# Attention and a routed expert layer on one core: the first units' plan cut in seven pieces, seven copies moved to ScalarE, four subtracts to GpSimd

## The chip, the cores and the metric

The kernel runs on one core of a Trainium2 chip. Its time is device microseconds from one execution, and several executions of the same program are shown. A core has TensorE (PE; its weight loads are shown apart as PEld), VectorE (DVE), ScalarE (ACT), GpSimd (POOL) and SyncE (SP), which only issues transfers here. Each engine works through its own queue in order, and waits by semaphores for what others produce. Lower is better.

## What is computed

Attention over 4 sequences of 768 tokens with 8 heads of 64, in which a token sees the 96 tokens up to itself and 8 global ones; then each of the 3072 rows of 512 goes to the one of 8 experts that a small gate chooses, and is multiplied by its gate weight:

```python
scores = scale * q @ k.T - slope * dist          # kept: is_global | is_local
a = softmax(scores); x = (a @ v) as rows [3072, 512]
logits = x @ w_gate + modality_bias[modality_id]
e_idx = argmax(logits); gate_w = softmax(logits)[e_idx]
for e in range(8):
    out[e_idx == e] = gate_w * (relu(x[e_idx == e] @ w1[e]) @ w2[e])
```

All is float32. w1 is 8 x 512 x 1024 and w2 is 8 x 1024 x 512.

## The kernel before

**Attention** goes over 24 blocks of 128 tokens (NBLK), 6 to a sequence (NB), in steps n = 0 to 24 of the function `step`. A step is a software pipeline: it makes the scores of block n on TensorE (`s_mm`), reduces them on VectorE with the bias table (`red`, L276, name sc) and exponentiates them on ScalarE (L287, pr); it transposes the probabilities of block n-1 on TensorE (`t_mm`, L301, tile pt, four pairs of heads, two PSUM buffers) and copies them to SBUF (`t_cp`, tile pT: pairs 0, 2 and 3 on VectorE, L310, pair 1 on ScalarE, L308); it multiplies by the values of block n-2 (`pv`), scales them (`rinv`, tile rin, L345; `xr`) and stores them in the DRAM buffer x_rows; and it transposes the queries and keys of block n+1 (`k_mm`, `k_cp`: qt on VectorE, kt on ScalarE, L228). GpSimd copies value rows meanwhile (`copyv`, L135, L137, L142: vo, vl).

**Routing.** The gate (`gate_a`, `gate_b`, `gate_c`) runs one to two steps later. When a sequence is complete, `route_a` to `route_d` give each token a place in a list sorted by expert: pks and pos (positions; the adds run on GpSimd, L427 to L433, but for the last sequence), pf and pi (as integers, VectorE), and `route_c` scatters the tokens to the DRAM list ids_sorted by indirect transfers from GpSimd's queue (L450), six to a sequence.

**Experts.** A unit is 256 rows of one expert. Its matmuls work on numbers split in a high and a low part: `split` makes of the raw weights a rounded copy on ScalarE (L661, ah for w1, bh for w2) and the remainder on VectorE (L662, al, bl), four pieces of 128x1024 for each matrix. `l1_unit` multiplies by w1 in groups of twelve matmuls, four pieces times three products (L690 to L692, phe); the last of the twelve reads the fourth piece's low part. `l2` multiplies by w2.

The first three units (eslots, NE = 3) are filled from the first two sequences alone, so that they can start before attention ends. Their **plan** needs the counts of these sequences: which expert each unit has (uei), from which place of the list (uoi), which rows are empty (inv), and how many units each expert has used (first_used, needed only by the later plan). `plan_e` runs it in four parts, by `items` and `slots`, on VectorE at the ends of steps 17, 18, 18 and 19 (LAST = 18). Then the weights of unit 0 are loaded (`ld_w`, SP's queue), the units' row numbers (`ld_x`, tile ui), and the rows gathered (`gather_x`, L628, xge, GpSimd's queue).

**What sets the order.** The dictionary `todo` holds what is done at the end of which step (`at(n, f)`). For TensorE, and in attention for ScalarE and VectorE, the order is as written. For GpSimd and SP a scheduler sets it at build time, by its own estimate of when things are ready. After step 24 the first groups of unit 0 are written among the last blocks' work (`l1_first`), then a loop runs over all units.

Of the kernel before, what the change touches and what calls it, by code (L numbers as in the profile page):

```python
# [67 lines left out]
def moe_attention_kernel(ctx, tc, q, k, v, n_global, n_local, modality, w_gate, mod_bias, w1, w2, out):  # L68
# [396 lines left out]
        scat.append(ins)  # L465


    def items(tag, pool, cnt, used, ni, first):

        def pl(name, shape, dt=F32):
            return pool.tile([P] + shape, dt, name=f"{name}{tag}")

        left = cnt
        if used is not None:
            left = pl("left", [E])
            V.scalar_tensor_tensor(left, used, -float(U), cnt, ALU.mult, ALU.add)
        ci = pl("ci", [E], I32)
        V.tensor_copy(ci, left)  # L480
        full = pl("full", [E])
        V.tensor_scalar(ci, ci, 8, None, ALU.logical_shift_right)
        V.tensor_copy(full, ci)
        t88 = pl("t88", [E, E])
        V.tensor_tensor(t88, le, bm(full, E), ALU.mult)
        cin = pl("cin", [E])
        V.reduce_sum(cin, t88, axis=AX.X)
        cex = pl("cex", [E])
        V.tensor_sub(cex, cin, full)
        if first:  # L490

            V.tensor_scalar(first_used, cex, -1.0, float(first), ALU.mult, ALU.add)
            V.tensor_scalar(first_used, first_used, 0.0, None, ALU.max)
            V.tensor_tensor(first_used, first_used, full, ALU.min)
        yield
        uc = bc(uidx[:, 0:ni], E)
        m1 = pl("m1", [ni, E])
        m2 = pl("m2", [ni, E])
        st = pl("st", [ni, E])
        V.tensor_tensor(m1, bm(cin, ni), uc, ALU.is_gt)  # L500
        V.tensor_tensor(m2, bm(cex, ni), uc, ALU.is_gt)
        V.tensor_sub(m1, m1, m2)
        V.tensor_tensor(st, uc, bm(cex, ni), ALU.subtract)
        V.tensor_mul(st, st, m1)
        yield
        if not first:
            rem = pl("rem", [E])
            V.scalar_tensor_tensor(rem, full, -float(U), left, ALU.mult, ALU.add)  # L508
            key = pl("key", [E])
            V.scalar_tensor_tensor(key, rem, 8.0, erev, ALU.mult, ALU.add)  # L510
            V.tensor_tensor(t88, bm(key, E), bc(key, E), ALU.is_gt)
            rr = pl("rr", [E])
            V.reduce_sum(rr, t88, axis=AX.X)
            V.tensor_scalar(rr, rr, cin[:, E - 1 : E], None, ALU.add)
            V.tensor_scalar(key, rem, 0.0, 1000.0, ALU.is_equal, ALU.mult)
            V.tensor_add(rr, rr, key)
            yield
            V.tensor_tensor(m2, bm(rr, ni), uc, ALU.is_equal)
            V.tensor_add(m1, m1, m2)
            V.tensor_tensor(m2, m2, bm(full, ni), ALU.mult)  # L520
            V.tensor_add(st, st, m2)
            if used is not None:
                V.tensor_tensor(m2, m1, bm(used, ni), ALU.mult)
                V.tensor_add(st, st, m2)
            yield
# [129 lines left out]
    def split(s, which, c, early=False):  # L655
        raw = s.raw.pop((which, c))
        nb = 2 if which == "b" and s.straight else 1
        pool = wspb if which == "b" or early else wsp
        th = pool.tile([P, 1024], F32R, tag=f"{which}h{c}{early}", name=f"{which}h{s.name}{c}", bufs=nb)
        tl = pool.tile([P, 1024], F32R, tag=f"{which}l{c}{early}", name=f"{which}l{s.name}{c}", bufs=nb)  # L660
        nc.scalar.copy(th, raw)  # L661
        V.tensor_sub(tl, raw, th.bitcast(F32))  # L662
# [262 lines left out]
    def at(n, f, *args):  # L925
        todo.setdefault(n, []).append((f, args))
# [135 lines left out]
    eslots, slist, grs = [], [], []  # L1062
    moe = {}

    def planned_e(r):
        uei, uoi, inv = slots("e", plan, *r, NE, 2)
        for u in range(NE):
            eslots.append(mk(f"e{u}", uei[0:1, u : u + 1], uoi[0:1, u : u + 1], inv[:, :, u], xd[0 : BE * S, :], 2))

    def plan_e(g=[]):  # L1070
        if not g:
            g.append(items("e", plan, base[:, BE - 1, NB, :], None, NE, NE))
        run("e", g[0], planned_e)

    for j in range(4):
        at(LAST - 1 + (0, 1, 1, 2)[j], plan_e)

    def open_moe():
        nonlocal wraw, wsp, xgp, idp, mp
# [8 lines left out]
    at(LAST + 1, open_moe)  # L1088
    at(LAST + 1, lambda: ld_w(eslots[0], "a", (0, 1)))
    at(LAST + 2, lambda: ld_w(eslots[0], "a", (2, 3)))  # L1090
    at(LAST + 3, lambda: [ld_x(s) for s in eslots])
    at(LAST + 4, lambda: [gather_x(s) for s in eslots[:GE]])
    for j in range(4):
        at(LAST + (3, 4, 5, 6)[j], split, None, "a", j)
# [26 lines left out]
    def step(n):  # L1121

        on, more, back = n < NBLK, n + 1 < NBLK, 0 < n <= NBLK
        load(n)
        if on:
            s_mm(n, 0)
            s_mm(n, 1)
            if not n:
                k_mm(1, 0)
                k_mm(1, 1)  # L1130
            for hh in (0, 2, 1, 3, 4, 6, 5):
                red(n, hh)
                if not n and hh == 3:
                    k_cp(1, 0)
                    k_cp(1, 1)
        if n > 1:
            rinv(n - 2)
            pv(n - 2)
        if back:
            t_mm(n - 1, 0)  # L1140
            t_cp(n - 1, 0)
            t_mm(n - 1, 1)
            t_cp(n - 1, 1, True)
        if on:
            red(n, 7)
        if n > 1:
            xr(n - 2)
        if n > 2:
            gate_a(*gates(n - 3))
        if back:  # L1150
            t_mm(n - 1, 2)
            t_cp(n - 1, 2)
        if more and n:
            k_mm(n + 1, 1)
            k_mm(n + 1, 0)
            k_cp(n + 1, 1)
            k_cp(n + 1, 0)
        if back:
            t_mm(n - 1, 3)
            t_cp(n - 1, 3, not on)  # L1160
            copyv(n - 1)
        if n > 3:
            gate_c(*gates(n - 4))
        for f, args in todo.pop(n, []):
            if f is split:
                args = (eslots[0],) + args[1:]
            f(*args)
        if n > 2:
            gate_b(*gates(n - 3))
# [26 lines left out]
    def rest():  # L1196
        for n in sorted(todo):
            for f, args in todo[n]:
                f(*args)
                if f is not route_c or args[1] == NB - 1:  # L1200
                    yield
        r = yield from items("b", plan, base[:, B - 1, NB, :], first_used, NI, 0)
        uei, uoi, inv = slots("b", plan, *[t[:, 0:NS] for t in r], NS, 2)
        for u in range(NS):
            slist.append(mk(f"s{u}", uei[0:1, u : u + 1], uoi[0:1, u : u + 1], inv[:, :, u], xd, 2))
        yield
        gr = yield from granules(*r)
# [170 lines left out]
```

## Time and profile before

| | |
|---|---|
| runs shown | 502.31, 501.94, 502.28 us, median 502.28 |
| profiled execution | 504.03 us, its span 502.2 us |
| mean granted TensorE clock | 0.987 |
| busy: PE, DVE, ACT, POOL | 468.6, 343.1, 297.5, 156.3 us |
| steps 17 to 24 | about 125 to 185 us |
| first matmul of unit 0 | 188.33 us |

Times in rows of the profile are microseconds from the start of the span. In a row of the timeline stand start, length, engine, line, operation, what it writes and reads, its shape, and in square brackets how long the engine stood idle before it and what ended that. "issue" means that the profile shows nothing that it waited for.

### The profile page before, as it was taken

The page shows a single profiled execution, that of the slowest core. Times are in us where ns is not written, and L with a number is a line of the kernel's source. Part 1 is how long each engine was busy: PE and PEld are TensorE (multiplying, and loading weights), DVE is VectorE, ACT ScalarE, POOL GpSimd, SP SyncE. Part 2 cuts the span into 40 slices and gives each one's busy share as a digit, 9 for nine tenths or more (in the row PEclk, how much of TensorE's full clock was granted, in tenths as well). Part 3 has the DMA queues.
Part 4 walks back from the last instruction along what each step waited for, and adds up shares of the span by engine and source line. Part 5 has one row for each costly group of instructions (what it writes and reads, how often), then busy time and mean ns, then how long its engine had stood idle before and what let it go on. Part 6 is the DMA issues. An engine that isn't in the chain of part 4 may idle for free.

```text
span 502.2 us, 15068 instructions
## 1 busy us (share of the span) xinstructions
PE 468.6 (93%) x5789; PEld 419.4 (84%) x5789; DVE 343.1 (68%) x999; ACT 297.5 (59%) x716; POOL 156.3 (31%) x234
## 2 busy tenths in 40 slices
PE   7879899999898989999999999899999999999991
PEld 6778899999787869898989898798988998798980
DVE  5868788978987874997756477474765748556530
ACT  6747777777667763546456466464665557555420
POOL 9513314545443355062130405204041040500100
PEclk9989999999989999999999999999999999999997
DMA  9778878787668934767785849778598666965100
GB/s 175 152 215 206 200 168 215 180 196 192 158 160 248 287 128 150 265 188 246 232 277 199 275 154 325 246 220 292 159 332 269 205 248 218 321 225 165 44 22 26
DMA packets 125509, 102.75 MB, mean 205 GB/s; under 512 B 96283, under 2 KB 97715, under 8 KB 125428
## 3 DMA queue, kind: packets, MB, share of 16 engines
q1 hardware_dynamic: 120660, 88.65, 60.8%
q0 software_dynamic: 4768, 13.05, 7.2%
q8 instruction: 47, 0.77, 0.6%
q14 instruction: 34, 0.28, 0.2%
HBM read 87.31 MB, written 14.63 MB: 203 GB/s over the span
## 4 chain that ended last, share of the span: by engine, by line
PE 44%; issue 12%; DVE 2%; DMA 2%; POOL 1%; ACT 0%; SPq 0%; POOLq 0%; DVEq 0%; ACTq 0%
PE phs L692 5%; PE phs L690 4%; PE phs L691 4%; PE pos L730 4%; PE pos L729 4%; PE pos L728 4%; PE phe L690 2%; PE phe L691 2%; PE phe L692 2%; PE poe L728 2%; PE poe L730 2%; PE poe L729 2%; DMA uig<-ids_sorted 2%; POOL out L744 1%; PE mts L673 1%
## 5 line engine op out<-in xcount | busy, mean ns | idle before, releaser
L287 ACT ACTIVATE pr<-sc,nmx 128x168 f32<-128x168 f32 x192 | 81.1, 423 | 30.5 <-DVE nmx L276 29.4
L692 PE MATMUL phs<-xhs,als 128*128 128x256 f32 x256 | 72.5, 283 | 0.6 <-DVE als L662 0.5
L690 PE MATMUL phs<-xhs,ahs 128*128 128x256 f32 x256 | 72.2, 282 | 0.0
L691 PE MATMUL phs<-xls,ahs 128*128 128x256 f32 x256 | 72.1, 282 | 0.0
L628 POOL DMA_INDIRECT xgs<-x_rows,uis x16 | 27.1, 1694 | 131.5 <-DMA uis<-ids_sorted 66.9
L276 DVE CUSTOM_DVE_ANT_0 sc<-s,tbl 128x168 f32<-128x168 f32 x192 | 52.1, 327 | 9.4 <-PE s L257 9.4
L697 DVE SCALAR_TENSOR_TENSOR hls<-phs,hhs 128x512 fp32r<-128x512 f32 x32 | 22.1, 692 | 51.0 <-ACT hhs L696 51.0
L301 PE MATMUL pt<-ident,pr 128*128 128x128 f32 x288 | 47.2, 288 | 7.3 <-DVE pT L310 4.7
L728 PE MATMUL pos<-bhs,hhs 128*128 128x512 f32 x128 | 51.4, 401 | 0.0
L730 PE MATMUL pos<-bhs,hls 128*128 128x512 f32 x128 | 50.6, 395 | 0.0
L729 PE MATMUL pos<-bls,hhs 128*128 128x512 f32 x128 | 50.5, 395 | 0.0
L692 PEld LDWEIGHTS phs<-xhs,als 128*128 128x128 f32 x256 | 48.8, 191 | 1.0 <-DVE als L662 1.0
L310 DVE COPY pT<-pt 128x384 f32<-128x384 f32 x71 | 38.9, 548 | 15.5 <-PE pt L301 15.4
L690 PEld LDWEIGHTS phs<-xhs,ahs 128*128 128x128 f32 x256 | 48.9, 191 | 0.4
L691 PEld LDWEIGHTS phs<-xls,ahs 128*128 128x128 f32 x256 | 48.8, 191 | 0.3
L696 ACT ACTIVATE hhs<-phs 128x512 fp32r<-128x512 f32 x32 | 19.1, 597 | 50.0 <-PE phs L692 50.0
L257 PEld LDWEIGHTS s<-kt,qt 64*64 64x64 f32 x1536 | 38.2, 132 | 10.4 <-ACT kt L228 6.1
L257 PE MATMUL s<-kt,qt 64*64 64x128 f32 (+1 forms) x1536 | 41.7, 248 | 4.7 <-ACT kt L228 1.8
L301 PEld LDWEIGHTS pt<-ident,pr 128*128 128x128 f32 x288 | 32.4, 144 | 13.1 <-DVE pT L310 5.4
L450 POOL DMA_INDIRECT ids_sorted<-tki,pi x24 | 25.4, 1060 | 34.7 <-DVE remb L508 17.6
L287 ACT ACTIVATION_READ_ACCUMULATOR pr<-sc,nmx 128x1 f32 x192 | 35.9, 187 | 0.0
L744 POOL DMA_INDIRECT out<-obs,ois x16 | 17.1, 1069 | 47.7 <-ACT obs L743 44.6
(343 smaller groups left out, 1251.2 us busy)
## 6 DMA issues: line engine op xcount, KB each, us to landing
va<-in_v SPq DMA_DIRECT2D x25, 256.0 KB, 4.2
kn<-in_k SPq DMA_DIRECT2D x24, 256.0 KB, 4.0
qn<-in_q SPq DMA_DIRECT2D x24, 256.0 KB, 5.0
x_rows<-xr SPq DMA_DIRECT2D x24, 256.0 KB, 3.7
vl<-in_v SPq DMA_DIRECT2D x84, 32.0 KB, 3.0
rawe0a<-in_moe_w SPq DMA_DIRECT2D x4, 512.0 KB, 5.9
rawe0b<-in_moe_w SPq DMA_DIRECT2D x4, 512.0 KB
rawe1a<-in_moe_w SPq DMA_DIRECT2D x4, 512.0 KB, 3.5
```

The lines of the kernel that those rows point to most:

```text
L257: nc.tensor.matmul(ps[h][64 * half : 64 * half + 64, c : c + cnt], qt[hs, hp, 64 * half : 64 * half + 64], keys, start=True, stop=True,)
L276: V.tensor_tensor_reduce(out=sc, in0=pss[n, hp // 2][h][:, hp % 2 * W : (hp % 2 + 1) * W], in1=(tbl0 if n % NB == 0 else tbl)[:, hh, :], o ...
L287: last[0] = nc.scalar.activation(pr[:, h * (PRW - W) : h * (PRW - W) + W], sc, AF.Exp, bias=nmx[:, hh : hh + 1], scale=-1.0, accum_out=sum ...
L301: nc.tensor.transpose(tp[:, j * P : (j + 1) * P], pr[:, o : o + P], ident)
L310: V.tensor_copy(pT.rearrange("p a b -> p (a b)"), tp[:, 0 : 3 * P])
L628: nc.gpsimd.indirect_dma_start(out=s.xg[:, t, :], out_offset=None, in_=s.xsrc, in_offset=bass.IndirectOffsetOnAxis(ap=s.ui[:, t, 0:1], axi ...
L690: nc.tensor.matmul(o, hi[:, fs], s.xh[:, c, :], start=(c == 0), stop=False)
L691: nc.tensor.matmul(o, hi[:, fs], s.xl[:, c, :], start=False, stop=False)
L692: nc.tensor.matmul(o, lo[:, fs], s.xh[:, c, :], start=False, stop=(c == 3))
L728: nc.tensor.matmul(s.po[t], s.hh[:, fc, tt], hi[:, wv], start=(fc == 0), stop=False)
L729: nc.tensor.matmul(s.po[t], s.hh[:, fc, tt], lo[:, wv], start=False, stop=False)
L730: nc.tensor.matmul(s.po[t], s.hl[:, fc, tt], hi[:, wv], start=False, stop=(fc == 7))
```

## The change

The plan of the first units is a function of its own now, in seven pieces with a `yield` behind each. Pieces 1, 3, 5 and 7 run at the ends of steps 17, 18, 19 and 21, and pieces 2, 4 and 6 in the middle of steps 18, 19 and 20, between the values' products of block n-2 and the first transposes' copy. The units are made as soon as their experts are known, and their list places and empty rows are filled in later. In steps 9, 11, 15 and 17 to 20 the third pair's copy goes to ScalarE. The low part of the four w1 pieces of unit 0 is subtracted by GpSimd. The text asks for the row numbers one step earlier.

```diff
     def split(s, which, c, early=False):
...
         nc.scalar.copy(th, raw)
-        V.tensor_sub(tl, raw, th.bitcast(F32))
+        (nc.gpsimd if which == "a" and s is eslots[0] else V).tensor_sub(tl, raw, th.bitcast(F32))
...
-    def planned_e(r):
-        uei, uoi, inv = slots("e", plan, *r, NE, 2)
-        for u in range(NE):
-            eslots.append(mk(f"e{u}", uei[0:1, u : u + 1], uoi[0:1, u : u + 1], inv[:, :, u], xd[0 : BE * S, :], 2))
-    def plan_e(g=[]):
-        if not g:
-            g.append(items("e", plan, base[:, BE - 1, NB, :], None, NE, NE))
-        run("e", g[0], planned_e)
-    for j in range(4):
-        at(LAST - 1 + (0, 1, 1, 2)[j], plan_e)
+    def plan_e():
...
+        V.tensor_copy(ci, cnt)
+        V.tensor_scalar(ci, ci, 8, None, ALU.logical_shift_right)
+        V.tensor_copy(full, ci)
+        V.tensor_tensor(t88, le, bm(full, E), ALU.mult)
+        V.reduce_sum(cin, t88, axis=AX.X)
+        yield
+        V.tensor_sub(cex, cin, full)
...
+        V.tensor_tensor(m1, bm(cin, NE), uc, ALU.is_gt)
+        V.tensor_tensor(m2, bm(cex, NE), uc, ALU.is_gt)
+        V.tensor_sub(m1, m1, m2)
+        yield
...
+        V.tensor_tensor(m2, m1, bm(eidx, NE), ALU.mult)
+        V.reduce_sum(uex, m2, axis=AX.X)
+        V.tensor_copy(uei, uex)
+        for u in range(NE):
+            eslots.append(mk(f"e{u}", uei[0:1, u : u + 1], None, None, xd[0 : BE * S, :], 2))
+        yield
+        V.tensor_tensor(st, uc, bm(cex, NE), ALU.subtract)
+        V.tensor_mul(st, st, m1)
+        V.reduce_sum(ust, st, axis=AX.X)
+        V.tensor_scalar_mul(ust, ust, float(U))
+        yield
+        V.scalar_tensor_tensor(uof, uex, float(NT), ust, ALU.mult, ALU.add)
+        V.tensor_copy(uoi, uof)
...
+        yield
+        V.tensor_scalar(first_used, cex, -1.0, float(NE), ALU.mult, ALU.add)
+        V.tensor_scalar(first_used, first_used, 0.0, None, ALU.max)
+        V.tensor_tensor(first_used, first_used, full, ALU.min)
+        yield
...
+        V.tensor_tensor(m2, m1, bm(cnt, NE), ALU.mult)
+        V.reduce_sum(uli, m2, axis=AX.X)
+        V.tensor_scalar(inv[:, 0, :], ust, pidx, None, ALU.add)
+        V.tensor_scalar(inv[:, 1, :], ust, pidx, 128.0, ALU.add, ALU.add)
+        V.tensor_tensor(inv, inv, bm(uli, 2), ALU.is_ge)
+        V.tensor_scalar_mul(inv, inv, OOB)
...
+        yield
+    parts_e = plan_e()
+    mid = {}
+    at(LAST - 1, next, parts_e)
+    mid[LAST] = mid[LAST + 1] = mid[LAST + 2] = lambda: next(parts_e)
+    at(LAST, next, parts_e)
+    at(LAST + 1, next, parts_e)
+    at(LAST + 3, next, parts_e)
+    ACT2 = {NB + 3, NB + 5, 2 * NB + 3, 2 * NB + 5, LAST, LAST + 1, LAST + 2}
...
-    at(LAST + 3, lambda: [ld_x(s) for s in eslots])
+    at(LAST + 2, lambda: [ld_x(s) for s in eslots])
...
+        if n in mid:
+            mid[n]()
         if back:
             t_mm(n - 1, 0)
             t_cp(n - 1, 0)
...
-            t_cp(n - 1, 2)
+            t_cp(n - 1, 2, n in ACT2)
```

`items` loses its branch for the first units, and is otherwise as before.

How this moves the queues is shown at two places. The first is VectorE at the end of step 17 and the start of step 18; se, pf and pi belong to the routing, cie to first_used to the plan, sc18 are the scores of block 18. Before:

```order
L444 CAST pi1_3287<-pf1_3285 128x6
L480 CAST cie_3289<-base_208 128x8
L482 TENSOR_SCALAR cie_3289<-cie_3289 128x8
L483 CAST fulle_3291<-cie_3289 128x8
L485 TENSOR_TENSOR t88e_3294<-le_205,fulle_3291 128x64
L487 TENSOR_REDUCE cine_3296<-t88e_3294 128x8
L489 TENSOR_TENSOR cexe_3298<-cine_3296,fulle_3291 128x8
L492 TENSOR_SCALAR first_used_209<-cexe_3298 128x8
L493 TENSOR_SCALAR first_used_209<-first_used_209 128x8
L494 TENSOR_TENSOR first_used_209<-first_used_209,fulle_3291 128x8
L276 ISA sc18_0_3357,nmx18_3356<-s18_0_0_3319,tbl0_169 128x168
```

VectorE with the change, from the same pi on:

```order
L444 CAST pi1_3287<-pf1_3285 128x6
L1068 CAST cie_3289<-base_208 128x8
L1069 TENSOR_SCALAR cie_3289<-cie_3289 128x8
L1070 CAST fulle_3290<-cie_3289 128x8
L1071 TENSOR_TENSOR t88e_3291<-le_205,fulle_3290 128x64
L1072 TENSOR_REDUCE cine_3292<-t88e_3291 128x8
L276 ISA sc18_0_3353,nmx18_3352<-s18_0_0_3315,tbl0_169 128x168
```

Four of nine instructions of the plan no longer stand ahead of the scores of step 18; cexe is in the second piece and first_used in the sixth. The second piece, on VectorE in the middle of step 18, behind the seventh score and rin:

```order
L345 TENSOR_SCALAR rin16_3374<-sums16_2978 128x8
L346 RECIPROCAL rin16_3374<-rin16_3374 128x8
L1074 TENSOR_TENSOR cexe_3293<-cine_3292,fulle_3290 128x8
L1077 TENSOR_TENSOR m1e_3412<-cine_3292,uidx_204 128x24
L1078 TENSOR_TENSOR m2e_3413<-cexe_3293,uidx_204 128x24
L1079 TENSOR_TENSOR m1e_3412<-m1e_3412,m2e_3413 128x24
L310 COPY pT17_0_3422<-pt17_0_3418 128x384
```

The copy of the first transposes (pT17_0), which stood right behind rin, has four instructions ahead of it.

The second place is GpSimd's queue from step 22 to the end of attention: vo are value rows, base and pos the third sequence's positions, ids_sorted the scatters (pi2 the third sequence's, pi3 the fourth's), xge2 the rows of unit 2, ale00 to ale03 the four low parts of unit 0. Before:

```order
L135 COPY vo1_81<-va2_78 64x512
L137 COPY vo1_81<-va1_77 64x512
L135 COPY vo2_82<-va3_79 64x512
L137 COPY vo2_82<-va2_78 64x512
L427 TENSOR_TENSOR base_208<-base_208,pks2_4262 128x8 x6
L431 TENSOR_TENSOR pos2_4271<-pks2_4262,base_208 128x48
L429 COPY base_208<-base_208 128x8
L432 TENSOR_TENSOR pos2_4271<-pos2_4271,ebase_202 128x48
L433 TENSOR_TENSOR pos2_4271<-pos2_4271,oh2_4053 128x48
L450 DMA ids_sorted<-tki_206,pi2_4445 24832x16 x6
L628 DMA xge2_4758<-x_rows,uie2_4086 128x512 x2
L450 DMA ids_sorted<-tki_206,pi3_4900 24832x16 x6
```

GpSimd with the change (ale00 stands between the second and the third copy, just ahead of these rows):

```order
L137 COPY vo2_82<-va2_78 64x512
L427 TENSOR_TENSOR base_208<-base_208,pks2_4262 128x8 x2
L656 TENSOR_TENSOR ale01_4282<-rawe0a1_3688,ahe01_4281 128x1024
L427 TENSOR_TENSOR base_208<-base_208,pks2_4262 128x8 x4
L431 TENSOR_TENSOR pos2_4271<-pks2_4262,base_208 128x48
L429 COPY base_208<-base_208 128x8
L432 TENSOR_TENSOR pos2_4271<-pos2_4271,ebase_202 128x48
L433 TENSOR_TENSOR pos2_4271<-pos2_4271,oh2_4078 128x48
L656 TENSOR_TENSOR ale02_4448<-rawe0a2_3865,ahe02_4447 128x1024
L450 DMA ids_sorted<-tki_206,pi2_4445 24832x16 x6
L622 DMA xge2_4758<-x_rows,uie2_3900 128x512 x2
L656 TENSOR_TENSOR ale03_4538<-rawe0a3_3867,ahe03_4537 128x1024
```

Four subtracts have come into the queue: two ahead of the positions' end, one behind it, and the fourth behind the six scatters of pi2 and the two gathers of unit 2. TensorE's order is unchanged.

More of the change, by code (lines that the diff above doesn't have):

```diff
@@ L465, in route_c, with items @@
         scat.append(ins)
-    def items(tag, pool, cnt, used, ni, first):
+    def items(tag, pool, cnt, used, ni):
         def pl(name, shape, dt=F32):
@@ L489, in items @@
         V.tensor_sub(cex, cin, full)
[L490 to L494, printed above, removed]
         yield
@@ L505, in items @@
         yield
[L506 to L520, printed above, removed]
+        rem = pl("rem", [E])
+        V.scalar_tensor_tensor(rem, full, -float(U), left, ALU.mult, ALU.add)
+        key = pl("key", [E])
+        V.scalar_tensor_tensor(key, rem, 8.0, erev, ALU.mult, ALU.add)
+        V.tensor_tensor(t88, bm(key, E), bc(key, E), ALU.is_gt)
+        rr = pl("rr", [E])
+        V.reduce_sum(rr, t88, axis=AX.X)
+        V.tensor_scalar(rr, rr, cin[:, E - 1 : E], None, ALU.add)
+        V.tensor_scalar(key, rem, 0.0, 1000.0, ALU.is_equal, ALU.mult)
+        V.tensor_add(rr, rr, key)
+        yield
+        V.tensor_tensor(m2, bm(rr, ni), uc, ALU.is_equal)
+        V.tensor_add(m1, m1, m2)
+        V.tensor_tensor(m2, m2, bm(full, ni), ALU.mult)
+        V.tensor_add(st, st, m2)
+        if used is not None:
+            V.tensor_tensor(m2, m1, bm(used, ni), ALU.mult)
             V.tensor_add(st, st, m2)
[L522 to L525, printed above, removed]
+        yield
         ust = pl("ust", [ni])
@@ L1063, in moe_attention_kernel, with pl @@
     moe = {}
-    def planned_e(r):
-        uei, uoi, inv = slots("e", plan, *r, NE, 2)
-        for u in range(NE):
-            eslots.append(mk(f"e{u}", uei[0:1, u : u + 1], uoi[0:1, u : u + 1], inv[:, :, u], xd[0 : BE * S, :], 2))
-    def plan_e(g=[]):
-        if not g:
-            g.append(items("e", plan, base[:, BE - 1, NB, :], None, NE, NE))
-        run("e", g[0], planned_e)
-    for j in range(4):
-        at(LAST - 1 + (0, 1, 1, 2)[j], plan_e)
+    def plan_e():
+        def pl(name, shape, dt=F32):
+            return plan.tile([P] + shape, dt, name=f"{name}e")
+        cnt = base[:, BE - 1, NB, :]
+        ci, full, t88 = pl("ci", [E], I32), pl("full", [E]), pl("t88", [E, E])
+        cin, cex = pl("cin", [E]), pl("cex", [E])
+        V.tensor_copy(ci, cnt)
[5 more added lines that the diff above has]
+        V.tensor_sub(cex, cin, full)
+        uc = bc(uidx[:, 0:NE], E)
+        m1, m2, st = (pl(nm, [NE, E]) for nm in ("m1", "m2", "st"))
+        V.tensor_tensor(m1, bm(cin, NE), uc, ALU.is_gt)
+        V.tensor_tensor(m2, bm(cex, NE), uc, ALU.is_gt)
+        V.tensor_sub(m1, m1, m2)
+        yield
+        uex, uei = pl("uex", [NE]), pl("uei", [NE], I32)
+        V.tensor_tensor(m2, m1, bm(eidx, NE), ALU.mult)
+        V.reduce_sum(uex, m2, axis=AX.X)
+        V.tensor_copy(uei, uex)
+        for u in range(NE):
+            eslots.append(mk(f"e{u}", uei[0:1, u : u + 1], None, None, xd[0 : BE * S, :], 2))
+        yield
+        ust, uof, uoi = pl("ust", [NE]), pl("uof", [NE]), pl("uoi", [NE], I32)
+        V.tensor_tensor(st, uc, bm(cex, NE), ALU.subtract)
[6 more added lines that the diff above has]
+        for u in range(NE):
+            eslots[u].o_src = uoi[0:1, u : u + 1]
+        yield
+        V.tensor_scalar(first_used, cex, -1.0, float(NE), ALU.mult, ALU.add)
+        V.tensor_scalar(first_used, first_used, 0.0, None, ALU.max)
+        V.tensor_tensor(first_used, first_used, full, ALU.min)
+        yield
+        uli, inv = pl("uli", [NE]), pl("inv", [2, NE])
+        V.tensor_tensor(m2, m1, bm(cnt, NE), ALU.mult)
[4 more added lines that the diff above has]
+        V.tensor_scalar_mul(inv, inv, OOB)
+        for u in range(NE):
+            eslots[u].inv = inv[:, :, u]
+        yield
@@ L1201, in rest @@
                     yield
-        r = yield from items("b", plan, base[:, B - 1, NB, :], first_used, NI, 0)
+        r = yield from items("b", plan, base[:, B - 1, NB, :], first_used, NI)
         uei, uoi, inv = slots("b", plan, *[t[:, 0:NS] for t in r], NS, 2)
```

## The prediction

> **What bounds the kernel now.** I read the page's busy shares first, then the busy time by stretches, then who TensorE waited for, and last the rows of each engine, in order of time, at the places that the change touches. The busy shares and two stretches (columns: stretch, length, busy time of PE, PEld, DVE, ACT, POOL, the granted clock, DMA share, GB/s):
>
> ```profile
> PE 468.6 (93%) x5789; PEld 419.4 (84%) x5789; DVE 343.1 (68%) x999; ACT 297.5 (59%) x716; POOL 156.3 (31%) x234
> ...
> 190.00:195.00 5.00, 5.00 (x51) 4.30 (x50) 1.59 (x5) 1.51 (x4) 4.09 (x4) 1.00 0.61 180
> ...
> 200.00:300.00 100.00, 100.00 (x643) 90.03 (x643) 72.40 (x159) 55.05 (x71) 24.37 (x21) 1.00 0.70 230
> ```
>
> TensorE carries the kernel. In the second phase (the expert units, from about 188 us) it doesn't stop: 5.00 of 5.00 us and 100.00 of 100.00 us. What it waits for there, between 185 and 488 us, all told (total, times, longest):
>
> ```profile
> PE htg L716 <- DVE hlg L720: 3.1, 3, 1.0
> PE phs L692 <- DVE als L662: 0.5, 1, 0.5
> ```
>
> So a time lost or won before TensorE reaches the units comes out at the end nearly whole: nothing behind has more than 3.6 us of slack, and 3.1 of it belongs to each granule's own chain. The question is when TensorE can run the units' first matmuls.
>
> **The end of step 17.** VectorE's rows, then GpSimd's beside them:
>
> ```profile
> 132.11 0.17 DVE L480 CAST cie<-base 128x8 int32<-128x8 f32 x1
> ...
> 132.98 0.22 DVE L487 TENSOR_REDUCE cine<-t88e 128x8 f32<-128x64 f32 x1
> 133.24 0.17 DVE L489 TENSOR_TENSOR cexe<-cine,fulle 128x8 f32<-128x8 f32 x1
> 133.44 0.55 DVE L492 TENSOR_SCALAR first_used<-cexe 128x8 f32<-128x8 f32 x1
> 134.03 0.64 DVE L493 TENSOR_SCALAR first_used<-first_used 128x8 f32<-128x8 f32 x1
> 134.70 0.62 DVE L494 TENSOR_TENSOR first_used<-first_used,fulle 128x8 f32<-128x8 f32 x1
> 135.24 0.32 DVE L276 CUSTOM_DVE_ANT_0 sc<-s,tbl 128x168 f32<-128x168 f32 x1
> ```
>
> ```profile
> 133.36 1.28 POOL L142 COPY vl<-vg 8x512 f32<-8x512 f32 x2 [2.18 <-PE x L322]
> 134.69 0.60 POOL L135 COPY vo<-va 64x512 f32<-64x512 f32 x1
> 135.35 0.61 POOL L137 COPY vo<-va 64x512 f32<-64x512 f32 x1
> ```
>
> Two things are to be seen. The plan holds step 18's first score instruction (L276) back until 135.24. And the three first_used instructions, of the same 128x8 as the cexe row, take 0.55 to 0.64 us instead of 0.17, ending at 133.99, 134.67 and 135.32, where GpSimd's copies end (the two of its first row at 134.00 and 134.64, the next at 135.29): a small VectorE instruction with SBUF operands stands still while GpSimd copies. The score instruction, which reads PSUM, does not (0.32 us beside the copy of 135.35).
>
> The new first piece ends with cine, so scores start at 133.24: 2.0 us earlier. The second piece (four instructions, about 0.23 us each by the 1.13 us of the five rows from 132.11) now stands ahead of that step's first transpose copy:
>
> ```profile
> 137.32 0.51 DVE L310 COPY pT<-pt 128x384 f32<-128x384 f32 x1
> 137.88 0.88 PE L301 MATMUL pt<-ident,pr 128*128 128x128 f32 x3 [1.29 <-DVE pT L310]
> 141.69 0.17 DVE L500 TENSOR_TENSOR m1e<-cine,uidx 128x24 f32<-128x24 f32 x1
> 143.57 0.33 DVE L276 CUSTOM_DVE_ANT_0 sc<-s,tbl 128x168 f32<-128x168 f32 x1
> ```
>
> The copy stood 2.08 us behind the first score; now 2.08 + 0.9, and 0.6 more if the GpSimd copy of 135.35 holds the piece up: 136.2 to 136.8 against 137.32. TensorE, which waits for it, gains 0.5 to 1.1 us. At the end of step 18 eleven instructions (141.69 to 143.57) become three: 1.3 us more. At step 19's end seven become two, but TensorE is the bound there and I give nothing for it. Pieces four and six (four and three small instructions) lie in front of a copy again, 0.6 to 0.9 us, and eat some of the lead.
>
> **Seven copies to ScalarE.** Means of the two forms:
>
> ```profile
> L310 DVE COPY pT<-pt 128x384 f32<-128x384 f32 x71 | 38.9, 548 | 15.5 <-PE pt L301 15.4
> L308 ACT COPY pT<-pt 128x384 f32<-128x384 f32 x25 | 11.5, 460 | 10.1 <-PE pt L301 10.1
> ```
>
> VectorE loses 7 x 0.55 us, ScalarE gets 7 x 0.46, ahead of the key copy (kt, L228) that the next step's scores need. Where VectorE is late it helps by up to 0.5, where ScalarE is just in time it hurts as much; steps 9, 11, 15, 17 to 20 hold some of both. I take -0.4 in all, between -2 and +1. Term one, the attention loop up to step 21: -0.8 - 1.3 - 0.4 = **-2.5 us** (-4 to -1.5). Moving the plan's loads changes the order on SP, the weights' four 512 KB loads going ahead of one step's v loads; the row loads keep their place behind step 21's x_rows store, so I give nothing for it.
>
> **The four subtracts on GpSimd.** Its queue, and VectorE's at the same place:
>
> ```profile
> 176.65 0.61 POOL L137 COPY vo<-va 64x512 f32<-64x512 f32 x1 [5.88 <-DMA xge<-x_rows,uie]
> ...
> 178.66 1.59 POOL L427 TENSOR_TENSOR base<-base,pks 128x8 f32<-128x8 f32 x6
> ...
> 180.95 0.28 POOL L433 TENSOR_TENSOR pos<-pos,oh 128x48 f32<-128x48 f32 x1
> 185.35 1.06 POOL L450 DMA_INDIRECT ids_sorted<-tki,pi  x1 [4.13 <-ACT pT L308]
> 186.72 1.42 POOL L450 DMA_INDIRECT ids_sorted<-tki,pi  x1 [0.31 <-issue]
> ...
> 194.38 0.98 POOL L628 DMA_INDIRECT xge<-x_rows,uie  x1 [0.30 <-issue]
> 195.66 0.96 POOL L628 DMA_INDIRECT xge<-x_rows,uie  x1 [0.30 <-issue]
> ```
>
> ```profile
> 181.26 0.20 DVE L442 TENSOR_REDUCE pf<-pos 128x6 f32<-128x48 f32 x1 [1.71 <-POOL pos L433]
> ...
> 181.66 1.23 DVE L662 TENSOR_TENSOR ale<-rawe0a,ahe 128x1024 fp32r<-128x1024 f32 x1
> 182.80 0.17 DVE L345 TENSOR_SCALAR rin<-sums 128x8 f32<-128x8 f32 x1
> ...
> 183.12 0.51 DVE L310 COPY pT<-pt 128x384 f32<-128x384 f32 x1
> ```
>
> ```profile
> 188.33 0.36 PE L690 MATMUL phe<-xhe,ahe 128*128 128x256 f32 x1
> ...
> 189.83 0.28 PE L692 MATMUL phe<-xhe,ale 128*128 128x256 f32 x1
> ```
>
> GpSimd is free only at 176.65, when the gathers of the first units' rows have landed, and already there VectorE waits 1.71 us for it (pos). The order puts subtract 0 behind that copy, subtract 1 between the adds, both ahead of pos; subtract 2 behind pos; and subtract 3 behind the six scatters and the two gathers, which fill GpSimd from 185.35 to 196.62 (195.66 + 0.96). The last of the units' first twelve matmuls (188.33 to 189.83) reads subtract 3.
>
> The price of one, 128x1024, is in no row. The nearest:
>
> ```profile
> L427 POOL TENSOR_TENSOR base<-base,pks 128x8 f32<-128x8 f32 x18 | 3.6, 200 | 1.6 <-DVE pks L424 0.2
> L431 POOL TENSOR_TENSOR pos<-pks,base 128x48 f32<-128x48 f32 x3 | 0.8, 283 | 0.0
> L135 POOL COPY vo<-va 64x512 f32<-64x512 f32 x24 | 14.5, 604 | 49.2 <-DMA va<-in_v 15.1 <-PE lq L387 11.7 <-PE s L257 6.0
> ...
> L205 POOL TENSOR_SCALAR tbl<-mm 128x168 f32<-128x168 f32 x4 | 2.5, 632 | 0.1
> ```
>
> The copy gives 604 x 2 = 1.2 us as the low end (one operand), the 128x168 row 632 x 1024/168 = 3.9 us as the high end (its fixed part multiplied too). The two rows of the same operation differ by 83 ns for 40 elements, 2.08 ns each: 0.20 + 1016 x 0.00208 = 2.3 us, and I take that.
>
> [...]
>
> The chain, on the clock of before with term one in it: GpSimd's copy at 176.65 - 2.5 = 174.15. From it to the end of pos (181.23) were 4.58 us, now with two subtracts 4.58 + 4.6: 183.33 instead of 181.23. Subtract 2 follows at once, to 185.63; VectorE's small SBUF instructions behind pos (the cast pi, rin) stand still beside it, as first_used did. Then 0.1 for pi and the 0.32 from rin to the copy: 186.1 against 183.12, **+3.0**. VectorE's own subtract of 1.23 us is gone from there and that is counted in. The scatters wait for ScalarE's copy of the same step's last transpose, which comes as much later: 185.35 + 3.0, and with the same 11.27 us the gathers end at 199.6. Subtract 3 ends at 201.95, and the matmul of 189.83 starts then: **+12.1 us**. What VectorE saves by subtract 3 (1.23 us) doesn't count: TensorE waits for GpSimd longer.
>
> **The clock.** TensorE will have stood some 10 us. After its waits of step 18 the trace has (PEclk is the sixth value behind the length):
>
> ```profile
> 135.00:140.00 5.00, 2.75 (x14) 2.54 (x15) 4.61 (x24) 4.30 (x18) 0.90 (x2) 0.79 0.71 169
> 140.00:145.00 5.00, 5.00 (x146) 4.64 (x145) 3.96 (x25) 1.90 (x7) 1.99 (x2) 0.86 0.58 139
> ```
>
> That is 5 x 0.21 + 5 x 0.14 = 1.75 us of clock, a little of it while idle: **+1.5 us** (0 to 1.75, since it may fall into a wait). [...] This trace shows a drop where the longest wait is the 1.29 us of 137.88. [...]
>
> Sum: 12.1 (term one is in it) + 1.5 = +13.6 us. The profiled execution took 504.03 us, its span 502.2 and 1.8 around it; it would go to 517.6. The median of the runs shown, 502.28, lies 1.75 lower, and goes to **515.9 us**.
>
> **Rivals.**
> - The row lists come early enough that GpSimd is free a good while before 174 and pos isn't late. For it: the text loads them one step earlier. Against: on SP they stand where they stood, behind the scatters. Then the copy of 183.12 comes 2.5 + 1.1 us earlier, 179.5; scatters from 181.7 to 193.0, subtract 3 at 195.3: +5.5, with 1.5 of clock 509.3 us. 13 in 100, with a subtract near the copy's 1.2 us (4 x 1.1 = 4.4 less: 511.5) counted here.
> - VectorE and GpSimd hold each other up on both sides, and a subtract costs 3.9 us: 4 x 1.6 = 6.4 more, 522 us. For it: the rows of first_used. Against: VectorE mostly waits there. 11 in 100.
> - Faster: subtract 3 is done before TensorE asks, and only VectorE's relief counts: 502.28 - 2.5 - 1.1 = 498.7 us. It decides at 189.8 - 3.6 = 186.2 us, about when the first scatter is issued; the queue's order has eight transfers' issue of some 1.27 us ahead, so it needs them to be issued without GpSimd's time. 5 in 100.
> - The stall and the gain cancel within 0.2% (1 us, about what runs of this kernel can tell from no change): 3 in 100, of which 1 falls to slower.
>
> The forecast has 68. Slower: 68 + 13 + 11 + 1 = 93; same 2; faster 5. Range: low end with 1.2 us a subtract (-4.4), VectorE not held beside subtract 2 (-1.2), 1.5 more gain and no clock loss (-1.5): +5, 507.5; high end 522.
>
> **What would show it.** Right: GpSimd rows of 128x1024 at 2.3 us, one behind the gathers at 199 to 202 us; TensorE waiting some 10 us for it in the units' first matmuls, then a stretch below full clock; VectorE waiting 4 us and more for pos; step 18's scores near 133.2. Wrong: a subtract 3 ahead of the scatters in time, gathers landing before 172 us, or a TensorE that never stops around 190.

## The result and the profile after

The changed kernel takes 517.89 us, the median of five runs (515.98 to 522.04); the kernel before took 502.31 us beside it (501.94 to 504.25). The ratio is 1.0298, with an interval of 1.0256 to 1.0341: slower by 3.0%. Forecast were 515.9 us, with 507.5 to 522 as range. The execution shown below is the longest of the five: 522.04 us, its span 520.3, its mean granted clock 0.963.

One thing is needed for the numbers further down: five of the twelve comparisons (vec_subs, subs_alone, sub3_vec, sub3_only, subs_alone_again), all on one and the same chip, ran where the kernel before itself took 529 to 533 us, the other seven, on three other chips, where it took 503 to 505 us, so each kernel is judged by its ratio to the kernel before of its own comparison.

The busy shares answer to the first line of the forecast: TensorE is busy as long as before (472.2 against 468.6 us), in a longer span.

```profile
PE 472.2 (91%) x5789; PEld 421.9 (81%) x5789; DVE 336.5 (65%) x988; ACT 300.4 (58%) x723; POOL 162.1 (31%) x238
```

Whom TensorE waited for between 115 and 210 us (total, times, longest):

```profile
PE phe L686 <- POOL ale L656: 7.7, 1, 7.7
PE pt L301 <- DVE pT L310: 7.2, 1, 7.2
PE x L334 <- POOL vo L137: 2.9, 1, 2.9
```

Three waits, one behind the other, all of them ending in GpSimd's queue or in VectorE behind it. They add up to 17.8 us; before, the copy of step 24's first transposes (183.12) cost 1.63 us, and there was no wait for ale. GpSimd's queue, in order of time:

```profile
171.11 0.95 POOL L622 DMA_INDIRECT xge<-x_rows,uie  x1 [0.30 <-issue]
172.10 0.60 POOL L135 COPY vo<-va 64x512 f32<-64x512 f32 x1
179.20 0.61 POOL L137 COPY vo<-va 64x512 f32<-64x512 f32 x1 [6.50 <-DMA xge<-x_rows,uie]
179.90 2.36 POOL L656 TENSOR_TENSOR ale<-rawe0a,ahe 128x1024 fp32r<-128x1024 f32 x1
...
183.99 2.33 POOL L656 TENSOR_TENSOR ale<-rawe0a,ahe 128x1024 fp32r<-128x1024 f32 x1
...
188.01 0.28 POOL L433 TENSOR_TENSOR pos<-pos,oh 128x48 f32<-128x48 f32 x1
188.25 2.34 POOL L656 TENSOR_TENSOR ale<-rawe0a,ahe 128x1024 fp32r<-128x1024 f32 x1
193.74 1.05 POOL L450 DMA_INDIRECT ids_sorted<-tki,pi  x1 [3.15 <-ACT pT L308]
...
203.66 0.96 POOL L622 DMA_INDIRECT xge<-x_rows,uie  x1 [0.30 <-issue]
204.64 2.36 POOL L656 TENSOR_TENSOR ale<-rawe0a,ahe 128x1024 fp32r<-128x1024 f32 x1
```

The order is the one that was read from the code: two subtracts ahead of pos, one behind it, the fourth behind eight transfers' issue. VectorE at the same place:

```profile
188.32 0.20 DVE L442 TENSOR_REDUCE pf<-pos 128x6 f32<-128x48 f32 x1 [11.32 <-POOL pos L433]
188.63 1.99 DVE L444 CAST pi<-pf 128x6 int32<-128x6 f32 x1
190.53 0.16 DVE L345 TENSOR_SCALAR rin<-sums 128x8 f32<-128x8 f32 x1
190.72 0.20 DVE L346 RECIPROCAL rin<-rin 128x8 f32<-128x8 f32 x1
190.84 0.51 DVE L310 COPY pT<-pt 128x384 f32<-128x384 f32 x1
```

VectorE waits 11.32 us for pos, and the cast of six numbers a row takes 1.99 us: it ends at 190.62, where the subtract of 188.25 ends (190.59). In vec_subs_again (below), where no subtract runs beside it, the same cast takes 0.17. The reduction of 188.32, though it too lies beside that subtract, takes 0.20, as in before (181.26) and in vec_subs_again (178.64) with no subtract beside it, so the prediction's "a small VectorE instruction with SBUF operands stands still while GpSimd copies" is too broad. What decides which instruction is held the runs don't show.

TensorE's first transposes of step 24, its first matmuls of unit 0, and the granted clock (sixth value behind the length) over the three waits:

```profile
191.40 1.54 PE L301 MATMUL pt<-ident,pr 128*128 128x128 f32 x6 [7.24 <-DVE pT L310]
...
197.84 0.36 PE L684 MATMUL phe<-xhe,ahe 128*128 128x256 f32 x1
...
199.10 0.28 PE L685 MATMUL phe<-xle,ahe 128*128 128x256 f32 x1
207.06 0.58 PE L686 MATMUL phe<-xhe,ale 128*128 128x256 f32 x1 [7.67 <-POOL ale L656]
209.00 0.58 PE L684 MATMUL phe<-xhe,ahe 128*128 128x256 f32 x1
```

```profile
180.00:185.00 5.00, 4.17 (x42) 3.65 (x42) 0.00 (x0) 1.06 (x2) 4.78 (x6) 0.50 0.33 33
185.00:190.00 5.00, 0.00 (x0) 0.00 (x0) 1.58 (x2) 0.00 (x0) 4.69 (x10) 0.50 0.85 248
190.00:195.00 5.00, 3.60 (x22) 3.19 (x23) 2.69 (x8) 1.75 (x4) 1.64 (x2) 0.50 0.54 191
195.00:200.00 5.00, 4.38 (x85) 3.81 (x83) 3.63 (x8) 2.55 (x4) 3.99 (x4) 0.97 0.11 31
200.00:205.00 5.00, 0.00 (x0) 0.00 (x0) 0.00 (x0) 0.00 (x0) 4.07 (x5) 0.72 0.60 189
205.00:210.00 5.00, 2.94 (x17) 2.24 (x18) 0.00 (x0) 0.83 (x2) 2.00 (x1) 0.50 0.51 156
210.00:215.00 5.00, 5.00 (x39) 4.39 (x38) 1.24 (x7) 0.86 (x2) 0.00 (x0) 0.76 0.01 3
```

The twelfth matmul starts at 207.06 instead of 189.83, the thirteenth at 209.00 instead of 190.84.

### The profile page after: what moved, and what is told of

It is laid out like the page before. It is cut to its first block, busy times and chain, and to the rows that moved or that the text cites. A ratio compares the mean times of both kernels' runs of the same rounds, so it can differ in the third digit from the quotient of the medians.

```text
span 520.3 us, 15075 instructions
## 1 busy us (share of the span) xinstructions
PE 472.2 (91%) x5789; PEld 421.9 (81%) x5789; DVE 336.5 (65%) x988; ACT 300.4 (58%) x723; POOL 162.1 (31%) x238
## 4 chain that ended last, share of the span: by engine, by line
PE 47%; issue 11%; POOL 3%; DVE 1%; ACT 0%; POOLq 0%; DVEq 0%; ACTq 0%
PE phs L686 4%; PE phs L684 4%; PE phs L685 4%; PE pos L724 4%; PE pos L723 4%; PE pos L722 4%; PE phe L686 2%; PE phe L684 2%; PE phe L685 2%; PE poe L722 2%; PE poe L724 2%; PE poe L723 2%; POOL ids_sorted L450 1%; POOL out L738 1%; PE mts L667 1%
## 5 line engine op out<-in xcount | busy, mean ns | idle before, releaser
L622 POOL DMA_INDIRECT xgs<-x_rows,uis x16 | 24.9, 1554 | 130.9 <-DMA uis<-ids_sorted 67.2
L310 DVE COPY pT<-pt 128x384 f32<-128x384 f32 x64 | 35.1, 550 | 16.8 <-PE pt L301 16.4
L334 PE MATMUL x<-vo,pT 128*64 128x64 f32 x384 | 29.7, 233 | 6.6 <-issue 3.7
```

The costliest lines, as they stand in the source:

```text
L310: V.tensor_copy(pT.rearrange("p a b -> p (a b)"), tp[:, 0 : 3 * P])
```

## The experiments

All of them edit the changed kernel unless it is said otherwise. Each profiled execution gives five numbers, read from its rows: where GpSimd's copy behind the gathers starts (L137), where the twelfth matmul of unit 0 starts, the time between these two, the time from the thirteenth to the end of the span, and what SP waited for the list's scatters before it loaded the row numbers. The nine executions of the comparisons at 502 to 505 us (us; "subs" says which subtracts are on GpSimd):

| kernel | subs | ratio | copy | 12th | copy to 12th | 13th to end | SP for scatters |
|---|---|---|---|---|---|---|---|
| before | none | 1 | 176.65 | 189.83 | 13.18 | 311.4 | 2.3 |
| changed | 0 to 3 | 1.0298 | 179.20 | 207.06 | 27.86 | 311.3 | 3.4 |
| vec_subs_again | none | 1.0034 | 174.02 | 188.59 | 14.57 | 309.8 | 4.2 |
| sub3_vec_again | 0 to 2 | 1.0113 | 180.35 | 201.09 | 20.74 | 309.8 | 3.9 |
| sub3_only_again | 3 | 1.0148 | 179.28 | 200.42 | 21.14 | 311.5 | 4.4 |
| sub3_early | 0 to 3 | 1.0092 | 176.35 | 197.31 | 20.96 | 311.0 | 3.0 |
| plan_alone | none | 1.0043 | 174.78 | 189.43 | 14.65 | 310.1 | 3.7 |
| loads_as_before | none | 1.0033 | 173.32 | 186.50 | 13.18 | 310.6 | 2.3 |
| copies_alone | none | 1.0000 | 177.47 | 192.04 | 14.57 | 309.8 | 1.6 |

From the thirteenth matmul to the end all nine take 309.8 to 311.5 us. A loss of several microseconds is therefore decided before it; a difference of 1.7 us or less between two executions can also come from behind it. Each row is one execution, and not a typical one: those of vec_subs_again, plan_alone and loads_as_before are the shortest of their kernels, those of the changed kernel, sub3_vec_again and sub3_only_again the longest.

**The subtracts back on VectorE, and the parts of them.**

```diff
# vec_subs, vec_subs_again
-        (nc.gpsimd if which == "a" and s is eslots[0] else V).tensor_sub(...)
+        V.tensor_sub(...)
# sub3_vec, sub3_vec_again: ... which == "a" and c < 3 and s is eslots[0] ...
# sub3_only, sub3_only_again: ... which == "a" and c == 3 and s is eslots[0] ...
# subs_alone, subs_alone_again: before.py with the line of the changed kernel
```

> The changed kernel with its four subtracts back on VectorE; plan, copies and loads as changed. Theory (the attention loop won some 2.5 us by plan and copies, and all of the loss is the subtracts on GpSimd): faster than before by 2.5 to 3.5 us, 498.8 to 499.8; TensorE waits for no ale, and its unit matmuls start 2 to 3 us before 188.3. Rival (the lead ends in a wait for GpSimd, whose value copy and position adds stand behind the gathers, and these landed 2.5 us later in the changed kernel, not earlier): 501.5 to 503, with VectorE waiting 4 us or more for pos.

> The kernel before with its four w1 subtracts of unit 0 on GpSimd, and nothing else. Theory (the loss and the gain add up): 2.5 us slower than the changed kernel, 519.5 to 521. Rival (once GpSimd is behind, the end of the gathers sets the time and the lead of the loop is worth nothing): 517 to 518.5, as the changed kernel.

> The changed kernel with the fourth subtract alone back on VectorE; the first three stay on GpSimd. Theory (two stalls one behind the other: the positions late by three subtracts, 2.9 and 7.2 us, and the fourth subtract behind the scatters, 7.7 us): the second stall goes, with about 1 us of low clock behind it and 1.2 us of VectorE's time in its place, so 509.5 to 511.5. Rival (the whole loss comes from the fourth one's place, and the late positions are hidden): 501 to 503. Second rival (VectorE standing still beside GpSimd is what counts): 515 or more.

> The changed kernel with only the fourth subtract on GpSimd; the first three are back on VectorE. Theory: the positions are as early as without any, the stalls of 2.9 and 7.2 us go, and the fourth still ends behind six scatters and two gathers, 2.4 us after them, near 198 to 200; TensorE waits some 9 us for it: 508 to 511. Rival (the scatters go out early enough once the positions are early): 500 to 503.

Measured, with the kernel before at 533.32 us: vec_subs 0.9882 (0.9824 to 0.9940), subs_alone 1.0152 (1.0093 to 1.0210), sub3_vec 1.0010 (0.9965 to 1.0055), sub3_only 0.9968 (0.9926 to 1.0011). The times in us of all four expectations failed, and the prices can't be read here, since TensorE itself was late. Its waits between 100 and 210 us in vec_subs:

```profile
PE s L257 <- issue: 6.3, 16, 1.0
PE x L334 <- issue: 1.9, 5, 0.5
```

In the trace of before, the same stretch has one issue stall, of 1.7 us; vec_subs has 24 and subs_alone_again 25. What causes them no run here shows. With TensorE late, GpSimd's late subtracts are partly covered: in subs_alone the twelfth matmul (213.07) has no wait listed, in subs_alone_again it waits 0.98 us for the fourth subtract, and in the changed kernel 7.67. Only the direction is taken from here, not its size: by the ratios vec_subs and subs_alone lie 2.7% apart (1.0152 / 0.9882), by the medians of all their runs, 530.98 and 534.96 us, 0.7%. Three were then run again.

> The kernel of vec_subs once more, since in that comparison the kernel before itself took 533 us, and in the trace of each kernel TensorE lost time in many short issue stalls from step 13 on; there the attention loop itself was the bound and GpSimd was never far behind. Theory (the loop won 2.5 us, and the subtracts on GpSimd are the whole loss): where the kernel before takes 502 to 505 us, a ratio of 0.993 to 0.996. Rival (the lead ends in the wait for the gathers and pos): 0.999 to 1.002. If the kernel before takes 530 us again: the ratio of the first comparison, 0.982 to 0.994.

Measured: 1.0034 (1.0000 to 1.0067), 506.4 against 504.08 us. That is a little above the rival's 0.999 to 1.002, and the theory is out: without GpSimd's subtracts the change is not faster. The subtracts cost 1.0298 - 1.0034, 2.6%, some 13 us (a difference of the ratios of two comparisons); the lead of plan and copies is worth nothing in the end.

> The kernel of sub3_vec once more (the changed kernel, its fourth subtract alone back on VectorE), for a comparison in which the kernel before takes 502 to 505 us. Theory (two stalls one behind the other; the one of 7.7 us at the fourth subtract goes, the ones of 2.9 and 7.2 us before step 24's transposes stay): against the changed kernel's ratio of 1.030 some 1.2 to 1.6 per cent less, a ratio of 1.013 to 1.018, and no wait of TensorE for ale. Rival (the late positions are hidden, all of it is the fourth one's place): 1.000 to 1.004.

> The kernel of sub3_only once more (the changed kernel with only the fourth subtract on GpSimd), for the same reason. Theory: positions, scatters and gathers as in vec_subs_again, whose gathers of unit 2 ended at 193.99; the subtract ends near 196.4, TensorE's matmul that reads it stood at 188.6: 7.8 us, and 1 to 1.5 of clock, on a ratio of 1.003: 1.019 to 1.023, with one wait of 6 to 8 us for ale. Rival (the stall is filled by other work or made good later): 1.003 to 1.008.

Measured: 1.0113 (1.0074 to 1.0152) and 1.0148 (1.0110 to 1.0185). Both lie below the theory's numbers and clearly above the rivals' (1.004 and 1.008). The traces show which stall is whose; sub3_vec_again first, sub3_only_again behind it, both from 160 to 230 us:

```profile
PE pt L301 <- DVE pT L310: 7.6, 1, 7.6
PE x L334 <- POOL vo L137: 1.5, 1, 1.5
```

```profile
PE phe L686 <- POOL ale L656: 6.4, 1, 6.4
PE x L334 <- POOL vo L137: 2.7, 1, 2.7
PE pt L301 <- DVE pT L310: 2.7, 2, 2.4
```

In the table's sixth column, against vec_subs_again, which differs from these kernels by the subtracts alone, the three early subtracts cost 20.74 - 14.57, 6.2 us, the fourth alone 6.6, all four 13.3: they add up, nearly. By the ratios it is 0.8 and 1.1 against 2.6%, and the intervals, some 0.4 each, leave open how nearly. The theory of sub3_only_again had its gathers where vec_subs_again has them; in its trace the copy behind them came 5.3 us later (179.28), with no subtract of GpSimd ahead of it.

**The queue's order alone.**

```diff
# sub3_early
-        at(LAST + (3, 4, 5, 6)[j], split, None, "a", j)
+        at(LAST + (3, 4, 5, 5)[j], split, None, "a", j)
```

> The changed kernel, all four subtracts on GpSimd, but the fourth piece's split is asked for one step earlier (step 23 with the third), which puts its subtract ahead of the six scatters and two gathers in GpSimd's queue. Theory (the 7.7 us stall is the queue's order, not the cost of 2.35 us): GpSimd stood 3.15 us idle ahead of the scatters, so the subtract fits; no wait of TensorE for ale, and VectorE's cast of the positions held some 2.4 us more at most: the ratio of sub3_vec_again, 1.011, or up to 0.005 above it. Rival (the subtracts' cost on GpSimd is what counts, wherever they stand): 1.026 to 1.034, as the changed kernel.

Measured: 1.0092 (1.0051 to 1.0132), the theory. GpSimd does the same four subtracts, the fourth now ahead of the scatters:

```profile
185.39 4.65 POOL L656 TENSOR_TENSOR ale<-rawe0a,ahe 128x1024 fp32r<-128x1024 f32 x2
190.88 1.06 POOL L450 DMA_INDIRECT ids_sorted<-tki,pi  x1 [0.85 <-ACT pT L308]
```

The first scatter is issued 14.53 us behind the copy of 176.35, in sub3_vec_again 14.54 (180.35 to 194.89): the fourth subtract costs nothing there, since it takes 2.3 of the 3.15 us that GpSimd stood idle. VectorE's cast is held for 1.99 us, as in the changed kernel, and not for a second subtract. TensorE waits for no ale, and copy to twelfth matmul goes from 27.86 to 20.96. So some 2 of the 3% were the queue's order, not the subtract's duration. (The edit moves the fourth piece's rounded copy on ScalarE up with the subtract; in the changed kernel no wait of GpSimd or TensorE is for that copy.)

**Plan and copies alone.**

```diff
# plan_alone: subtracts on VectorE, ACT2 = set(), ld_x at LAST + 3
# loads_as_before: plan_alone, and
-    mid[LAST] = mid[LAST + 1] = mid[LAST + 2] = lambda: next(parts_e)
-    at(LAST, next, parts_e)
+    mid[LAST] = mid[LAST + 2] = lambda: next(parts_e)
     at(LAST + 1, next, parts_e)
+    at(LAST + 1, next, parts_e)
+    at(LAST + 3, next, parts_e)
     at(LAST + 3, next, parts_e)
# copies_alone: before.py with ACT2 and t_cp(n - 1, 2, n in ACT2)
```

> The changed kernel with the subtracts on VectorE, all third-pair copies on VectorE and the row numbers asked for where they were: the seven-piece plan alone. Theory (the plan wins 2 us at steps 18 to 20, the copies to ScalarE cost a little or nothing): a ratio of 0.994 to 0.998. Rival (what the plan wins at step 18 ends in later gathers, as the weights' loads now start some 5 us earlier and the scatters of the list land later): 0.999 to 1.004, as vec_subs_again, with GpSimd's copy behind the gathers no earlier than 176.65 on the clock of the kernel before.

Measured: 1.0043 (1.0011 to 1.0076). The theory is out, and the ratio lies just above the rival's 0.999 to 1.004. One part of the rival's sign did not come: the copy behind the gathers stands at 174.78, ahead of 176.65. The trace still shows a lead that shrinks. VectorE's rin of steps 17 and 21 in before, then in plan_alone:

```profile
126.88 0.22 DVE L345 TENSOR_SCALAR rin<-sums 128x8 f32<-128x8 f32 x1
...
158.24 0.25 DVE L345 TENSOR_SCALAR rin<-sums 128x8 f32<-128x8 f32 x1
```

```profile
127.62 0.22 DVE L345 TENSOR_SCALAR rin<-sums 128x8 f32<-128x8 f32 x1
...
156.28 0.17 DVE L345 TENSOR_SCALAR rin<-sums 128x8 f32<-128x8 f32 x1
```

The loop wins 2.70 us here (28.66 instead of 31.36). By rin plan_alone leads by 1.96 us at step 21 and by 2.88 at steps 22 and 23; the copy behind the gathers leads by 1.87, rin of step 24 by 1.86, the twelfth matmul by 0.40. Between the last two lie step 24's wait and the clock behind it:

```profile
177.34 0.27 PE L334 MATMUL x<-vo,pT 128*64 128x64 f32 x1 [0.48 <-POOL base L427]
181.83 1.48 PE L301 MATMUL pt<-ident,pr 128*128 128x128 f32 x6 [2.10 <-DVE pT L310]
```

```profile
180.00:185.00 5.00, 3.17 (x21) 2.77 (x22) 3.32 (x9) 1.94 (x4) 0.90 (x1) 0.69 0.44 157
```

The wait is 0.47 longer than before's 1.63, and the clock, 1.00 in that stretch before, is 0.69: 5 x 0.31, at most 1.6 us, since part of it falls into the wait.

> plan_alone with the third and fourth piece of the plan moved to the end of step 19 and the last two to the end of step 21: the scores of step 18 are freed as in plan_alone, but the experts are known a step later, so that the four 512 KB weight loads stand behind step 19's loads of v in SP's queue, as in the kernel before. Theory (the lead of 2.9 us that plan_alone had at step 20 was lost since the weights' loads started at 141.4 instead of 149.9 us and held up the list's scatters, 5.5 against 2.1 us to land, and with them the row numbers, the gathers and GpSimd's copy behind them): the first scatters land within 2.5 us, the copy behind the gathers keeps the lead, and the time is 1.5 to 2.5 us below the kernel before, a ratio of 0.995 to 0.997. Rival (the lead is lost to something else, such as the clock after the wait at step 24 or issue stalls at step 13): 1.000 to 1.005, as plan_alone.

Measured: 1.0033 (0.9991 to 1.0075), 505.97 against 503.23 us: the rival's number. (By rin plan_alone's lead was 2.79 at step 20 and 2.88 at step 22.) The profiled execution did what the theory said: SP waits 2.3 us for the scatters as in before, the copy behind the gathers starts at 173.32, TensorE does not wait at step 24, and the twelfth matmul starts at 186.50, 3.3 us ahead of before. But that execution, 499.93 us, is the fastest of twelve, and the slowest took 509.71. So the theory fits one execution and fails for the time: over its runs this kernel isn't faster either, and the cause is not shown.

> The kernel before with the seven third-pair copies on ScalarE and nothing else. Theory (they help VectorE by up to 0.5 us where it is late and hold up the key copy where ScalarE is just in time): between -2 and +1 us, a ratio of 0.996 to 1.002. Rival (they are part of why the changed kernel's loop is no faster up to step 17, where it came 0.6 to 2 us later in the trace): 1.003 to 1.006.

Measured: 1.0000 (0.9962 to 1.0038), the theory. Seven copies on ScalarE are worth nothing that can be measured.

> The kernel of subs_alone once more (the kernel before with its four w1 subtracts of unit 0 on GpSimd and nothing else), for a comparison in which the kernel before takes 502 to 505 us. Plan, copies and loads were worth nothing measurable by themselves (1.004, 1.000, 1.003), so: theory (the subtracts are the whole loss): a ratio of 1.024 to 1.032, one wait of TensorE for ale of 6 to 9 us and one of 4 us or more for the first transposes' copy of step 24. Rival (the rest of the change made it worse, by the gathers' coming later): 1.012 to 1.020, with the copy behind the gathers at 176.7 and a wait of step 24 below 5 us.

Measured: 1.0119 (1.0022 to 1.0217), once more with a kernel before of 528.7 us, so that the condition it was written for did not hold. TensorE waits 1.0 us for ale and at most 1.3 for a transposes' copy, not 6 to 9 and 4, for the reason given with the first four. The subtracts by themselves at 502 to 505 us weren't measured; their price there is the difference between the changed kernel and vec_subs_again.

## Why the prediction was right, and where its steps were off

The forecast of 515.9 us was 2.0 below the median, and its mechanism is the one that the runs show: the subtracts on GpSimd, two stalls, the second from the fourth's place in the queue. That it came so near is partly luck. By the ratio of vec_subs_again the rest of the change costs 1.7 us (0 to 3.4) and does not win 2.5, and the subtracts with their clock some 13.3 us and not 16.1: errors of 4.2 and 2.8 us that largely cancel.

- **A subtract, 2.3 us.** 2.33 to 2.36 measured.
- **The chain behind the copy.** Forecast from copy to the end of the fourth subtract: 201.95 - 174.15, 27.80 us. Measured: 207.00 - 179.20, 27.80. Its inner steps hold as well: pos ends 9.2 us behind the copy by forecast and 9.1 in the trace, the first transposes' copy stands 11.95 and 11.64 behind, the first scatter 14.2 and 14.54, the gathers' end 25.45 and 25.42. The wait for the fourth subtract was put at some 10 us and is 7.67: from the start of step 24's first transposes TensorE needed 7.99 us to get there (191.40 to 199.39), at a clock of 0.50 in the 5 us from 190, against 6.15 before (183.68 to 189.83), so that this part of the clock's loss fell into the wait.
- **Term one, -2.5 us.** The loop did win it: from rin of step 17 to rin of step 21 before took 31.36 us, the changed kernel 28.73, 2.6 less:

```profile
129.00 0.21 DVE L345 TENSOR_SCALAR rin<-sums 128x8 f32<-128x8 f32 x1
...
157.73 0.57 DVE L345 TENSOR_SCALAR rin<-sums 128x8 f32<-128x8 f32 x1
```

What failed is that the gathers move with the loop, "176.65 - 2.5 = 174.15", because "the row loads keep their place". In the trace the copy behind them starts at 179.20, 5.05 later than forecast. Of this some 2 us were lost ahead of step 17 (129.00 against 126.88), where the trace has an issue stall of 1.44 us at 108.86 that the trace of before has not. The rest lies between step 21 and the copy: 21.47 us, against 18.41. There SP waited longer for the scatters (3.4 against 2.3 us), as in all six kernels that load the weights early (3.0 to 4.4, with 1.6 to 2.3 in the three that load them later). The weights' four 512 KB loads start at 145.07 instead of 149.94, since the experts are known earlier; "I give nothing for it" put these loads at nothing. That they are the cause isn't shown: SP's longer wait is 1.1 of these 3.1 us, and in vec_subs_again, with the loads earlier still (141.81) and a wait of 4.2 us, step 21 to the copy takes 17.47 us (156.55 to 174.02), less than before. What failed for the time is more than this: without GpSimd's subtracts the lead is not in the runs at all (1.0034).
- **The rest of the sum.** The clock was put at +1.5. Visible is 0.9: from the twelfth to the thirteenth matmul 1.94 us instead of 1.01. The 0.76 of 210 to 215 us lies in the table's seventh column, where it can't be told from the executions' other differences. What the clock took between the waits lies inside the chain. So the profiled execution's own sum is 2.55 (copy) + 14.68 (chain) + 0.93 (clock) - 0.06, 18.1 us, the 520.3 - 502.2 of the spans; the forecast had -2.5 + 14.6 + 1.5.
- **Not foreseen.** TensorE's wait of 2.90 us for the values copied behind the gathers: I had priced the queue's lateness at pos, but block 22's products need that copy first. It adds nothing: the transposes of step 24 start when VectorE's copy lets them, at 191.40, whenever those products were done.
- **The rivals.** Row lists early: no, the gathers came later. Subtracts of 3.9 us: no. Mutual hold-up: VectorE's cast stood still for 1.99 us as reckoned with, GpSimd's subtracts didn't grow (2.34 beside the cast, 2.33 to 2.36 the others). The fourth subtract done early would have needed another place in the queue, as sub3_early gave it; even then the rival's 498.7 us was not reached, because the positions remain late (VectorE waits 10.67 us for them, and TensorE then 7.70 for the first transposes' copy).

What stays open is why plan_alone and loads_as_before, whose profiled executions gain 1.7 and 4.1 us of span on the trace of before, are not faster over their runs. The runs of either spread over more than 9 us, and the profiled ones were the shortest of their series. Open too is why TensorE was late on the one chip.

## What to carry to other kernels

Before work is moved to an engine because it is idle, write out what stands ahead of it in that engine's queue and what stands behind: here one subtract of 2.35 us cost nothing ahead of the scatters and 7 us behind them. A lead won in a loop reaches the end only if everything that the next phase waits for moves with it; here the loop won 2.6 us, and the copy behind the gathers came 2.55 us later. And a price that was carried on from two rows of the same operation, of 8 and 48 elements, to 1024 elements held within 3% here.

## What the runs showed of the hardware

- TensorE's clock fell around a wait of about 2 us (2.10 in plan_alone, with 0.63 and 0.48 in the 7 us ahead of it; 0.69 in the 5 us around it) and stayed at 1.00 after one of 1.63 at the same place in before. The longest wait alone doesn't decide: in before it fell to 0.79 around the 1.29 and 1.1 us of step 18.
- Where the kernel before takes 502 to 505 us, issue stalls of TensorE of 0.3 to 2.5 us stand mostly at few fixed places of the program: the values' products of steps 7, 14 and 18 and the transposes of step 21 (59.90 and 160.64 in before; 60.28, 108.86, 137.10 and 159.14 in the changed kernel; where the text of loads_as_before says step 13, it is step 14), but a given execution has only some of them.
- An indirect transfer mostly occupies GpSimd for some 1.27 us (0.96 and 0.30 of issue; single ones up to 1.92 and 0.30), and the second copy behind the four gathers waits, by the profile, until they have landed: 5.88 us in before, 6.50 in the changed kernel, 4.67 to 6.50 in all nine traces of the table.
